# Two plane clears and the natural mask ahead of the first weights' issue on GpSimd, third weights and middle rows behind its first mask

## The chip, the cores and the metric

The kernel runs on one core of a Trainium2 chip. The metric is the device time of one execution in microseconds (us). Five engines work side by side and meet only through semaphores: TensorE (PE in the profile, PEld its weight loads), VectorE (DVE), ScalarE (ACT), GpSimd (POOL) and SyncE (SP), which here only issues transfers. Transfers run on 16 DMA engines that all issuers share: queue 0 holds what GpSimd issues, queue 1 what SyncE issues, queue 10 what ScalarE issues.

## What is computed

Two stages, for 4 batches, 8 heads, 768 tokens, head size 32 and state size 16 (the reference, cut to what matters):

```python
for c in range(24):                       # chunks of 32 tokens, one after the other
    cum = np.cumsum(log_a[chunk], axis=-1)
    M = einsum('bhin,bhjn->bhij', Cc, Bc) * exp(cum_i - cum_j) * causal
    y = einsum('bhij,bhjd->bhid', M, xc)  + einsum('bhin,bhnd->bhid', Cc, state) * exp(cum)
    state = exp(sum(la)) * state + sum_j(Bc * xc * exp(cum_last - cum_j))
x = y.transpose(0, 2, 1, 3).reshape(4 * 768, 256)
out = ((x @ w_a) * (x @ w_b)) @ w_out     # 256 -> 1536 -> 256
```

A scan over the sequence with a decaying state per head, then a bilinear feed-forward network (FFN) on 3072 tokens.

## The kernel before

The sequence is cut into 6 blocks of 128 tokens, each worked on in two pairs of batches, so that there are 12 pairs. Within a block the decay is a running product (`scan`, L250, on VectorE) that is divided by its value in the middle of the block (`over_mid`, L253) and multiplied into B and C. For a pair the scaled B and C are turned so that the state dimension lies on partitions, TensorE forms the scores (`scores`, L404, into four PSUM banks), the scores are multiplied with a causal mask (`mask`: L449 on VectorE, or L446 and L447, a copy by ScalarE and the product by GpSimd), and the masked scores are multiplied with x (`pv_u`, L458). The results are evacuated to X2T (block 0) or XB (later blocks) and go into the FFN: matmuls with Wa and Wb (L598 for block 0, L667 after it), the product of the two (L622, L679), and matmuls with Wo (L637, L693).

The order of the work is written out by hand from L774 on: the kernel takes a manual schedule, each engine carries out its instructions in the order of the text, and a wait holds everything behind it on that engine. Small matmuls on constants (`warmup`, L238) stand between TensorE's pieces in the first 10 us.

*Block 0* (pairs 0 and 1) goes a shorter way than the rest: B and C are loaded by pair, scaled on VectorE (`scale_bc`, L333), turned by TensorE (`transposes`, L374) and copied out (L385, L391). *Pairs 2 and later* use one interleaved buffer each, a plane (three in turn, `planes`), into which GpSimd writes scaled C and B (`scale_q`, L346) and which VectorE turns in one instruction (`turn`, L359). Part of each plane stays zero: `clear` (L294) writes those words once for each of the three planes. The factors of the planes come from the middle rows (`mid_rows`, L288: the running product over its middle value, on GpSimd), which VectorE turns (`turned_rows`, L297) and which are copied into FC and inverted into FB.

There are two masks. `causal` (L222, L225) is in the order of the first two blocks, whose tokens are interleaved by two; `causal_q` (L915, L916) is in natural order and is used from pair 4 on.

*Loads.* ScalarE and SyncE issue B and C of block 0 first, GpSimd issues x of pair 0 (L153), the first halves of Wa and Wb (L185), x of pair 1, then the second halves; Wa's second half ("third weights") at L234, ahead of everything that GpSimd computes, and Wb's second half ("fourth") at L814. The weights are converted to 16 bits by the transfer. SyncE then issues the eight loads of block 1 (`load_q`, L164: four of C into cq, four of B into bq), with a dependency written by hand on the first half of Wa, so that they don't start ahead of it (L815, L816). The loads of x and B for pairs 2 and 3 follow.

*PSUM banks.* Two double banks hold scores. Four more (ff0 to ff3) are handed out in order of use by the string `BANKS`; its first entries are, in order, fps, tb, tc, py0, py1, then three results with Wa and three with Wb for pair 0. A bank that is handed out again makes the new writer wait for the readers of the old content.

Of the kernel before, what the change touches and what calls it, by code (L numbers as in the profile page):

```python
# [12 lines left out]
u32 = mybir.dt.uint32  # L13
AF = mybir.ActivationFunctionType
ALU = mybir.AluOpType
# [4 lines left out]
SS = 64.0  # L20

BANKS = (
    "012313213212312312031203123021032103120312013201320130231021302130231203120312013023102310"
    "2312013201320132012301230123012301230123012301320132013201320132013201320132013201320"
)


# [1 line left out]
def kernel(  # L29
# [13 lines left out]
    nc = tc.nc  # L43
# [3 lines left out]
    Q = 128  # L47
# [30 lines left out]
    Wa = [big.tile([128, 2, KC], f16, name=f"Wa{t}") for t in range(2)]  # L78
# [6 lines left out]
    causal_q = big.tile([128, Q], f16, name="causal_q")  # L85
# [10 lines left out]
    planes = [big.tile([128, 288, 4], f16, name=f"planes{t}") for t in range(NR)]  # L96
# [32 lines left out]
    def bank(name):  # L129
        return psf.tile([128, 512], f32, name=name, tag=f"ff{next(banks)}")  # L130
# [12 lines left out]
    def load1(eng, p, which, bt, i0=0, n=64, to=None):  # L143
        blk, bp = divmod(p, NBP)
        if p >= P2:
            return eng.dma_start(
                by_token(pair_in[p][which])[:, bt],
                (B, C, x)[which][2 * bp + bt, :, blk * Q : (blk + 1) * Q, :].rearrange("h q n -> q h n"),
            )
        src = (B, C, x)[which][2 * bp + bt, :, blk * Q + 2 * i0 : blk * Q + 2 * i0 + 2 * n, :]  # L150
        if to is None:
            to = pair_in[p][which]
        return eng.dma_start(  # L153
            to[64 * bt + i0 : 64 * bt + i0 + n].rearrange("i h r n -> i h (r n)"),
            src.rearrange("h (i r) n -> i h (r n)", r=2),
        )
# [3 lines left out]
    def load_q(eng, blk, parts=ALL_Q):  # L160
        if blk not in by_batch:
            by_batch[blk] = [inq.tile([128, H, 4, N], f32, name=n_, tag=n_) for n_ in ("bq", "cq")]
        return [
            eng.dma_start(  # L164
                by_batch[blk][w][32 * b : 32 * b + 32].rearrange("i h s n -> i h (s n)"),
                (B, C)[w][b, :, blk * Q : (blk + 1) * Q, :].rearrange("h (i s) n -> i h (s n)", s=4),
            )
            for w, b in parts
        ]
# [12 lines left out]
    def load_w(half, W):  # L182
        src = moe_w_a if W is Wa else moe_w_b
        c = slice(half * KC, (half + 1) * KC)
        return nc.gpsimd.dma_start(W[half], src.rearrange("(f p) e -> p f e", p=128)[:, :, c])  # L185

    def load_wo(half):
# [2 lines left out]
            moe_w_out.rearrange("(g p kk) e -> p g (kk e)", p=128, kk=3)[:, 2 * half : 2 * half + 2],  # L190
        )

    nc.sync.dma_start(a_sb, a.rearrange("b h (k q) -> (b h) k q", q=Q))
    for p_ in range(2):
        tiles(p_)
# [5 lines left out]
    for w in (1, 0):  # L201
# [6 lines left out]
        out=ident, in_=ident, compare_op=ALU.is_equal, fill=0.0, base=0, pattern=[[-1, 128]], channel_multiplier=1  # L208
# [14 lines left out]
    for bt in range(2):  # L223
        v = causal[64 * bt : 64 * bt + 64]
        nc.gpsimd.affine_select(  # L225
            out=v, in_=v, compare_op=ALU.is_ge, fill=0.0, base=0, pattern=[[-1, 2], [1, Q]], channel_multiplier=-2
        )
    for p in range(2):
        for bt in range(2):
            load1(nc.gpsimd, p, 2, bt)  # L230
        if p == 0:
            w0 = load_w(0, Wa)
            load_w(0, Wb)
    load_w(1, Wa)  # L234

    def warmup(bank, *widths):
        for cols in widths:
            nc.tensor.matmul(  # L238
                bank[:, 0:cols],
                nc.const_aps.tensor(1.0, [128, 128], mybir.dt.bfloat16),  # L240
                nc.const_aps.tensor(1.0, [128, cols], mybir.dt.bfloat16),
                start=True,
                stop=True,
                skip_group_check=True,
            )


    def scan(lo, hi):
        for k in range(lo, hi):
            nc.vector.tensor_tensor_scan(Pr[:, k], a_sb[:, k], zero, 1.0, ALU.mult, ALU.add)  # L250
# [4 lines left out]
    def sel_over_mid(lo, hi, eng):  # L255
        eng.tensor_tensor(
            out=selr[:, lo:hi].rearrange("p k t c -> p k (t c)"),
            in0=sel.rearrange("p t b h -> p (t b h)").unsqueeze(1).broadcast_to((BH, hi - lo, 2 * NBP * H)),
            in1=rmid[:, lo:hi].unsqueeze(2).broadcast_to((BH, hi - lo, 2 * NBP * H)),
            op=ALU.mult,  # L260
        )
# [24 lines left out]
    def mid_rows(lo, hi, eng):  # L286
        k = slice(lo + NBLK - NT, hi + NBLK - NT)
        eng.tensor_tensor(  # L288
            out=Ps[:, lo:hi], in0=Pr[:, k], in1=rmid[:, k].unsqueeze(2).broadcast_to((BH, hi - lo, Q)), op=ALU.mult
        )  # L290

    def clear(t_, eng):
        words = t_.rearrange("p c s -> p (c s)").bitcast(u32).rearrange("p (g w) -> p g w", g=3)
        eng.memset(words[:, 0:2, 32:96], 0)  # L294

    def turned_rows(lo, hi):
        nc.vector.transpose(  # L297
# [26 lines left out]
    def scale_bc(p, which, eng, factor=None):  # L324
        blk, bp = divmod(p, NBP)
        name, f = (("bm", fB), ("cm", fC))[which]
        if p >= P2:
            f = (fBl, fCl)[which][:, blk - P2 // NBP].rearrange("p (b t h) -> p b t h", b=NBP, t=2)[:, bp]
        else:
            f = f[:, blk, :, bp]  # L330
        raw = by_token(pair_in[p][which]) if p >= P2 else pair_in[p][which].rearrange("p h r n -> p r h n")
        m_ = mid.tile([128, 2, H, N], f16, name=name, tag=name)
        eng.tensor_tensor(  # L333
            out=m_,
            in0=raw,
            in1=(f if factor is None else factor).unsqueeze(3).broadcast_to((128, 2, H, N)),
            op=ALU.mult,
        )
        st.setdefault(p, {})[name] = m_
# [94 lines left out]
    def product0(m2, e):  # L434

        return (
            st[0]["T1"][:, 2 * m2 : 2 * m2 + 2].rearrange("p m (e r) q -> p e m (r q)", e=2)[:, e],
            (SC0, SC1)[m2][:, :, e * 256 : e * 256 + 256],
            causal.rearrange("p r q -> p (r q)").unsqueeze(1).broadcast_to((128, 2, 2 * Q)),
        )  # L440

    def mask(out_in, by_pool=False):
        o_, i_, c_ = out_in
        if by_pool:
            tmp = mid.tile([128, *c_.shape[1:]], f32, name="tmp", tag="tmp")
            nc.scalar.copy(tmp, i_)  # L446
            nc.gpsimd.tensor_tensor(out=o_, in0=tmp, in1=c_, op=ALU.mult)  # L447
        else:
            nc.vector.tensor_tensor(out=o_, in0=i_, in1=c_, op=ALU.mult)  # L449

    def pv_u(p, u, py, first):
        s = st[p]
        for r in range(2):
            for g in range(4):
                for bt in range(2):
                    h = u * 4 + g
                    k = slice(64 * bt, 64 * bt + 64)
                    nc.tensor.matmul(  # L458
                        py[bt][32 * g : 32 * g + 32, u * Q : (u + 1) * Q],
                        s["X16"][k, h, r, :],  # L460
                        s["T1"][k, h // 2, h % 2 * 2 + r],
                        start=(first and u == 0 and r == 0),
                        stop=(r == 1),
                        skip_group_check=True,
                        tile_position=(64 * bt, 32 * g),
                    )
# [93 lines left out]
    def evac0(u, bt, eng, py):  # L560
        o_, i_ = X2T[:, 0, bt, u], py[bt][:, u * Q : (u + 1) * Q]
        if eng is nc.scalar:
            nc.scalar.activation(out=o_, in_=i_, func=AF.Copy, scale=YS / SS)
        else:
            nc.vector.tensor_scalar(o_, i_, YS / SS, None, ALU.mult)
# [218 lines left out]
    scale_bc(0, 1, nc.vector, v.rearrange("p (r b h) -> p r b h", r=2, b=NBP)[:, :, 0])  # L784
    over_mid(1, 2)
    sel_over_mid(1, 2, nc.vector)
    mid_rows(0, 1, nc.gpsimd)
    tb, tcp = bank("tb"), bank("tc")
    transposes(0, [tb, tcp], lambda: warmup(SC[3], 256))
    nc.scalar.copy(flat(fC, 0, 1), v)  # L790
# [3 lines left out]
    mask(product0(0, 0))  # L794
    mask(product0(0, 1))
    mask(product0(1, 1), by_pool=True)
    mask(product0(1, 0))
    clear(planes[0], nc.gpsimd)
    warmup(tcp, 512)
    factors_mm(1, 2, fps, 1)  # L800
    warmup(tcp, 512, 512)
# [3 lines left out]
        evac0(0, bt, nc.scalar, py)  # L805
    warmup(tcp, 512, 128)
    scale_bc(1, 1, nc.vector)
    scan(4, 5)
    scale_bc(1, 0, nc.vector)
    clear(planes[1], nc.gpsimd)  # L810
    pv_u(0, 1, py, True)
    for bt in range(2):
        evac0(1, bt, (nc.scalar, nc.vector)[bt], py)
    load_w(1, Wb)  # L814
    for i_ in load_q(nc.sync, 1):  # L815
        tc.add_manual_dep(i_.ins, w0.ins.name, AFTER, reason="first weights ahead of block 1")  # L816
    for p in (2, 3):
# [2 lines left out]
    for p in (2, 3):  # L820
# [10 lines left out]
        out=hsx,  # L831
# [11 lines left out]
    for m in range(3):  # L843
# [37 lines left out]
        out=Ge.rearrange("p k (g e) -> p g k e", e=2),  # L881
# [8 lines left out]
    for (p, k2), a_sb_ in zip(late, asb):  # L890
# [21 lines left out]
    batch_factors(1, 2, 2, 3)  # L912
    scale_bc(2, 0, nc.gpsimd)
    scale_bc(3, 0, nc.gpsimd)
    nc.gpsimd.memset(causal_q, SS)  # L915
    nc.gpsimd.affine_select(  # L916
        out=causal_q, in_=causal_q, compare_op=ALU.is_ge, fill=0.0, base=0, pattern=[[1, Q]], channel_multiplier=-1
    )
    for m in range(3):
        mask(product(3, m))  # L920
    batch_inverse(1, 2)
# [6 lines left out]
    for c in range(3):  # L928
        p, bt = divmod(c, NBP)
# [137 lines left out]
```

## Time and profile before

| | |
|---|---|
| runs shown: median (lowest to highest) | 122.97 us (122.58 to 123.0) |
| profiled execution: its own time | 122.69 us |
| its span | 120.8 us |
| busy: PE, DVE, ACT, POOL | 96%, 75%, 56%, 49% of the span |
| granted TensorE clock | 1.0 throughout |
| DMA engines' busy share, by fortieths of the span (3.02 us each) | 0.3 in the first, 0.9 or more in the next seven |

All times inside the profile count from the start of the span. Its time lines give start, length, engine, line, operation, written and read tiles, and in brackets how long the engine was idle before and what ended that. A busy PE is not one at its peak, since matmuls overlap and their ends are modelled; a wait is put down to the last of several semaphores. The three busiest groups outside TensorE, for the scale of things (line, engine, operation, tiles, shapes, count, then busy us, mean ns of one, and idle us before it):

```profile
L612 ACT COPY asb<-aps 128x512 f32<-128x512 f32 x72 | 42.0, 587 | 17.2 <-PE aps L667 13.4
L679 DVE TENSOR_TENSOR hkb<-bps,asb 128x512 f16<-128x512 f32 x60 | 40.2, 687 | 12.7 <-ACT asb L612 11.1
L449 DVE TENSOR_TENSOR t<-SC,causal_q 128x512 f16<-128x512 f32 x27 | 17.3, 681 | 2.4 <-PE SC L404 2.4
```

### The profile page before, as it was taken

What the parts mean: (1) busy time and instruction counts of PE and PEld (TensorE: products, weight loads), DVE (VectorE), ACT (ScalarE), POOL (GpSimd) and SP (SyncE); (2) the same over time, 40 slices, a digit from 0 to 9 for tenths busy, and PEclk for the clock granted to TensorE, in tenths of its full rate; (3) what the DMA queues carried; (4) which work ended last, traced back from release to release, by engine and by line L of the source; (5) the groups of instructions that cost most, each with busy time, mean ns of one, the idle gap of its engine ahead of it and who ended that gap; (6) DMA issues with size and microseconds to landing.
All of it is one profiled execution on the core that took longest, in us unless ns stands there. A gap on an engine that the chain in (4) does not pass through costs nothing.

```text
span 120.8 us, 3551 instructions
## 1 busy us (share of the span) xinstructions
PE 115.9 (96%) x1385; PEld 73.9 (61%) x1386; DVE 90.2 (75%) x166; ACT 67.9 (56%) x136; POOL 58.8 (49%) x92
## 2 busy tenths in 40 slices
PE   7989999999999999999999999999999999999990
PEld 2436789888644488544485464775465684645880
DVE  5998988999798994599966999686899426758000
ACT  0446756769776646567666646635735637475230
POOL 7994986999699969387803994200000000000000
PEclk9999999999999999999999999999999999999999
DMA  3999999894789994959992929012001111010132
GB/s 63 135 183 192 207 230 197 134 200 113 99 94 161 115 139 101 110 68 121 218 241 89 85 9 121 5 46 87 5 6 40 43 49 44 0 43 0 43 108 71
DMA packets 59297, 12.13 MB, mean 100 GB/s; under 512 B 54480, under 2 KB 59216, under 8 KB 59280
## 3 DMA queue, kind: packets, MB, share of 16 engines
q0 software_dynamic: 20320, 3.80, 38.9%
q1 hardware_dynamic: 36432, 7.74, 34.8%
q10 hardware_dynamic: 2528, 0.36, 1.8%
q8 instruction: 11, 0.18, 0.7%
q14 instruction: 6, 0.05, 0.1%
HBM read 12.42 MB, written 3.15 MB: 129 GB/s over the span
## 4 chain that ended last, share of the span: by engine, by line
PE 92%; DVE 4%; issue 0%; ACT 0%
PE ops L693 22%; PE aps L667 22%; PE bps L667 21%; PE ops L637 5%; PE aps L598 4%; PE SC L404 4%; PE bps L598 3%; DVE t L449 3%; PE SC L238 3%; PE SC L473 2%; PE SC L536 1%; PE tc L238 1%; PE py L458 1%; PE SC L485 1%; DVE bt L385 1%
## 5 line engine op out<-in xcount | busy, mean ns | idle before, releaser
L612 ACT COPY asb<-aps 128x512 f32<-128x512 f32 x72 | 42.0, 587 | 17.2 <-PE aps L667 13.4
L679 DVE TENSOR_TENSOR hkb<-bps,asb 128x512 f16<-128x512 f32 x60 | 40.2, 687 | 12.7 <-ACT asb L612 11.1
L667 PE MATMUL aps<-XB,Wa 128*128 128x512 f16 x120 | 35.7, 379 | 0.0
L667 PE MATMUL bps<-XB,Wb 128*128 128x512 f16 x120 | 35.7, 379 | 0.0
L693 PE MATMUL ops<-Wo,hkb 128*128 128x256 f16 (+1 forms) x252 | 28.1, 268 | 0.0
L693 PEld LDWEIGHTS <-hkb 128*128 128x128 f16 x252 | 23.0, 98 | 3.8
L667 PEld LDWEIGHTS <-Wb 128*128 128x128 f16 x120 | 12.4, 103 | 13.6
L667 PEld LDWEIGHTS <-Wa 128*128 128x128 f16 x120 | 12.1, 103 | 11.7 <-issue 0.5
L449 DVE TENSOR_TENSOR t<-SC,causal_q 128x512 f16<-128x512 f32 x27 | 17.3, 681 | 2.4 <-PE SC L404 2.4
L705 ACT ACTIVATE osb<-ops 128x256 f32<-128x256 f32 (+1 forms) x20 | 7.6, 379 | 18.4 <-PE ops L693 18.4
L447 POOL TENSOR_TENSOR t<-tmp,causal_q 128x512 f16<-128x512 f32 x5 | 5.8, 1161 | 10.0 <-ACT tmp L446 10.0
L177 POOL DMA_DIRECT2D xn<-in_x_dram x8 | 9.5, 1192 | 0.0
L346 POOL TENSOR_TENSOR planes<-cq,FC 128x256 f16<-128x256 f32 x10 | 7.6, 775 | 2.2 <-DMA cq<-in_C_dram 2.1
L622 DVE TENSOR_TENSOR hk<-bps,asb 128x512 f16<-128x512 f32 x11 | 7.2, 672 | 0.9 <-ACT asb L612 0.8
L346 POOL TENSOR_TENSOR planes<-bq,FB 128x256 f16<-128x256 f32 x10 | 7.7, 772 | 0.4 <-DMA bq<-in_B_dram 0.4
L449 DVE TENSOR_TENSOR t<-SC,causal 128x512 f16<-128x512 f32 x11 | 7.0, 675 | 0.4 <-PE SC L404 0.3
L598 PE MATMUL aps<-X2T,Wa 128*128 128x256 f16 x48 | 6.8, 274 | 0.0
L446 ACT COPY tmp<-SC 128x512 f32<-128x512 f32 x10 | 5.9, 589 | 1.5 <-PE SC L404 1.1
L598 PE MATMUL bps<-X2T,Wb 128*128 128x256 f16 x48 | 6.6, 273 | 0.0
L558 ACT ACTIVATE XB<-SC 128x512 f16<-128x512 f32 (+1 forms) x9 | 4.6, 547 | 3.5 <-PE SC L501 2.4
L447 POOL TENSOR_TENSOR t<-tmp,causal 128x512 f16<-128x512 f32 x5 | 5.8, 1161 | 0.0
L637 PE MATMUL ops<-Wo,hk 128*128 128x256 f16 x48 | 5.8, 273 | 0.0
(101 smaller groups left out, 109.2 us busy)
## 6 DMA issues: line engine op xcount, KB each, us to landing
out_dram<-osb SPq DMA_DIRECT2D x23, 128.0 KB, 1.8
cq<-in_C_dram SPq DMA_DIRECT2D x20, 64.0 KB, 3.9
bq<-in_B_dram SPq DMA_DIRECT2D x18, 64.0 KB, 3.8
bn<-in_B_dram SPq DMA_DIRECT2D x8, 128.0 KB, 4.1
xn<-in_x_dram POOLq DMA_DIRECT2D x8, 128.0 KB, 5.9
Wa<-in_moe_w_a_dram POOLq DMA_DIRECT2D x2, 384.0 KB, 7.3
Wb<-in_moe_w_b_dram POOLq DMA_DIRECT2D x2, 384.0 KB, 7.9
Wo<-in_moe_w_out_dram POOLq DMA_DIRECT2D x2, 384.0 KB, 6.5
```

Of the source, the lines that this page charges most:

```text
L177: eng.dma_start(by_token(pair_in[p][which]).rearrange("p t h n -> p (t h) n"), src.rearrange("t h q n -> q (t h) n"))
L346: eng.tensor_tensor(out=plane[:, c0 : c0 + 4 * step].rearrange("p (j c) s -> p j s c", c=step)[:, :, :, 0:N], in0=by_batch[blk][which][:, ...
L447: nc.gpsimd.tensor_tensor(out=o_, in0=tmp, in1=c_, op=ALU.mult)
L449: nc.vector.tensor_tensor(out=o_, in0=i_, in1=c_, op=ALU.mult)
L598: nc.tensor.matmul(ps[:, kk * 2 * Q : (kk + 1) * 2 * Q], W[k // 6][:, f, k % 6 // 3 * 384 : (k % 6 // 3 + 1) * 384].rearrange("p (c kk) -> ...
L612: (nc.vector.tensor_copy if on_dve else nc.scalar.copy)(asb, a_ps)
L622: eng.tensor_tensor(out=s["hk"][:, 2 * k2 : 2 * k2 + 2, :].rearrange("p k q -> p (k q)"), in0=b_ps, in1=asb, op=ALU.mult)
L637: nc.tensor.matmul(o_ps[:, 0:d_model], hk[:, k, bt * Q : (bt + 1) * Q], Wo[:, k, :], start=(k == 0), stop=(k == NK - 1), skip_group_check= ...
L667: nc.tensor.matmul(t_, W[k // 6][:, f, k % 6 // 3 * 384 : (k % 6 // 3 + 1) * 384].rearrange("p (c kk) -> p kk c", kk=3)[:, k % 3], XB[:, b ...
L679: return lambda: nc.vector.tensor_tensor(out=s["hk"][:, k], in0=ps[1], in1=asb, op=ALU.mult)
L693: nc.tensor.matmul(o_ps[:, 0:w], hk[:, k, c * Q : (c + 1) * Q], Wo[:, k, cs], start=(k == 0), stop=(k == NK - 1), skip_group_check=True,)
L705: nc.scalar.activation(out=o_sb[:, 0:w], in_=o_ps[:, 0:w], func=AF.Copy, scale=1.0 / (YS * YS))
```

## The change

Five moves, with no instruction added or taken away:

- GpSimd clears planes 0 and 1 and builds `causal_q` (memset and select) right after x of pair 0, ahead of the first halves of Wa and Wb. Before, the clears stood behind its first mask, and `causal_q` stood ahead of pair 3's masks.
- The third weights go from ahead of GpSimd's computing to behind its first mask. The fourth stay next after the clears' old places and so come right behind the third.
- The middle rows of block 1 go from ahead of the first mask to behind the fourth weights.
- On VectorE the scan of block 4 goes from ahead of pair 1's scaling of B to behind its evacuation of pair 0's second result (L565).
- `BANKS` has other digits. Followed through, all but two handings-out get a bank with the same history as before: the second and the third Wa result of pair 0 exchange theirs (the banks of tc and of py1).

`clear` itself is only moved up in the text.

```diff
--- before.py
+++ after.py
@@ -20,8 +20,8 @@
 SS = 64.0
 
 BANKS = (
-    "012313213212312312031203123021032103120312013201320130231021302130231203120312013023102310"
-    "2312013201320132012301230123012301230123012301320132013201320132013201320132013201320"
+    "012313123121321321032103213012031203210321023102310230132012301230132103210321023013201320"
+    "1321023102310231021302130213021302130213021302310231023102310231023102310231023102310"
 )
 
 
@@ -189,6 +189,10 @@
             Wo[:, 6 * half : 6 * half + 6].rearrange("p (g kk) e -> p g (kk e)", kk=3),
             moe_w_out.rearrange("(g p kk) e -> p g (kk e)", p=128, kk=3)[:, 2 * half : 2 * half + 2],
         )
+
+    def clear(t_, eng):
+        words = t_.rearrange("p c s -> p (c s)").bitcast(u32).rearrange("p (g w) -> p g w", g=3)
+        eng.memset(words[:, 0:2, 32:96], 0)
 
     nc.sync.dma_start(a_sb, a.rearrange("b h (k q) -> (b h) k q", q=Q))
     for p_ in range(2):
@@ -229,9 +233,14 @@
         for bt in range(2):
             load1(nc.gpsimd, p, 2, bt)
         if p == 0:
+            clear(planes[0], nc.gpsimd)
+            clear(planes[1], nc.gpsimd)
+            nc.gpsimd.memset(causal_q, SS)
+            nc.gpsimd.affine_select(
+                out=causal_q, in_=causal_q, compare_op=ALU.is_ge, fill=0.0, base=0, pattern=[[1, Q]], channel_multiplier=-1
+            )
             w0 = load_w(0, Wa)
             load_w(0, Wb)
-    load_w(1, Wa)
 
     def warmup(bank, *widths):
         for cols in widths:
@@ -288,10 +297,6 @@
         eng.tensor_tensor(
             out=Ps[:, lo:hi], in0=Pr[:, k], in1=rmid[:, k].unsqueeze(2).broadcast_to((BH, hi - lo, Q)), op=ALU.mult
         )
-
-    def clear(t_, eng):
-        words = t_.rearrange("p c s -> p (c s)").bitcast(u32).rearrange("p (g w) -> p g w", g=3)
-        eng.memset(words[:, 0:2, 32:96], 0)
 
     def turned_rows(lo, hi):
         nc.vector.transpose(
@@ -784,7 +789,6 @@
     scale_bc(0, 1, nc.vector, v.rearrange("p (r b h) -> p r b h", r=2, b=NBP)[:, :, 0])
     over_mid(1, 2)
     sel_over_mid(1, 2, nc.vector)
-    mid_rows(0, 1, nc.gpsimd)
     tb, tcp = bank("tb"), bank("tc")
     transposes(0, [tb, tcp], lambda: warmup(SC[3], 256))
     nc.scalar.copy(flat(fC, 0, 1), v)
@@ -794,8 +798,8 @@
     mask(product0(0, 0))
     mask(product0(0, 1))
     mask(product0(1, 1), by_pool=True)
+    load_w(1, Wa)
     mask(product0(1, 0))
-    clear(planes[0], nc.gpsimd)
     warmup(tcp, 512)
     factors_mm(1, 2, fps, 1)
     warmup(tcp, 512, 512)
@@ -805,13 +809,13 @@
         evac0(0, bt, nc.scalar, py)
     warmup(tcp, 512, 128)
     scale_bc(1, 1, nc.vector)
-    scan(4, 5)
     scale_bc(1, 0, nc.vector)
-    clear(planes[1], nc.gpsimd)
     pv_u(0, 1, py, True)
     for bt in range(2):
         evac0(1, bt, (nc.scalar, nc.vector)[bt], py)
+    scan(4, 5)
     load_w(1, Wb)
+    mid_rows(0, 1, nc.gpsimd)
     for i_ in load_q(nc.sync, 1):
         tc.add_manual_dep(i_.ins, w0.ins.name, AFTER, reason="first weights ahead of block 1")
     for p in (2, 3):
@@ -912,10 +916,6 @@
     batch_factors(1, 2, 2, 3)
     scale_bc(2, 0, nc.gpsimd)
     scale_bc(3, 0, nc.gpsimd)
-    nc.gpsimd.memset(causal_q, SS)
-    nc.gpsimd.affine_select(
-        out=causal_q, in_=causal_q, compare_op=ALU.is_ge, fill=0.0, base=0, pattern=[[1, Q]], channel_multiplier=-1
-    )
     for m in range(3):
         mask(product(3, m))
     batch_inverse(1, 2)
```

## The prediction

> **What bounds the kernel now.** I read the page first, then the chain of waits in order of time, then GpSimd's and SyncE's own rows, and last the DMA queues in narrow windows, because the change moves four DMA issues. On the page the chain that ended last is TensorE for 92% and VectorE for 4%.
>
> ```profile
> PE 92%; DVE 4%; issue 0%; ACT 0%
> ```
>
> In the chain, VectorE stands almost only before 14 us: from 14.85 on the pieces are TensorE's. So the change can pay or cost in two ways: in the short latency chain before 14 us, and by opening holes in TensorE afterwards. The chain around the change:
>
> ```profile
> 9.21 0.47 PE py L458 x16
> 9.68 0.54 PE tc L238 x2
> 10.22 0.32 PE SC L374 x4
> 10.54 0.87 PE aps L598 x8
> 11.41 0.47 PE SC L404 x32
> 11.88 0.04 issue
> 11.91 1.90 DVE t L449 x3
> ```
>
> To be seen: the first FFN matmuls (aps) want the first weights at 10.4, and the three causal masks of pair 1 are the last VectorE piece. The timeline of GpSimd over the moved stretch (start, length, then line, operation, tiles):
>
> ```profile
> 4.06 0.72 POOL L185 DMA_DIRECT2D Wa<-in_moe_w_a_dram  x1
> 4.76 0.73 POOL L185 DMA_DIRECT2D Wb<-in_moe_w_b_dram  x1
> 5.47 1.41 POOL L153 DMA_DIRECT2D xn<-in_x_dram  x2
> 6.83 0.76 POOL L185 DMA_DIRECT2D Wa<-in_moe_w_a_dram  x1
> 7.65 0.39 POOL L288 TENSOR_TENSOR Ps<-Pr,rmid 32x128 f32<-32x128 f32 x1
> 8.01 1.15 POOL L447 TENSOR_TENSOR t<-tmp,causal 128x512 f16<-128x512 f32 x1
> 9.11 0.34 POOL L294 MEMSET planes<- 128x128 uint32 x2
> 9.40 0.76 POOL L185 DMA_DIRECT2D Wb<-in_moe_w_b_dram  x1
> ```
>
> GpSimd never idles there, so what is put ahead of the first weights delays them in full. Who waits for them: SyncE's list of waits, and GpSimd's.
>
> ```profile
> SPq L164 <- DMA Wa<-in_moe_w_a_dram: 5.1, 1, 5.1
> ```
>
> ```profile
> POOL planes L346 <- DMA cq<-in_C_dram: 1.4, 1, 1.4
> ```
>
> SyncE holds block 1's eight loads until the first weights have landed, and GpSimd's planes wait for them. VectorE's rows show what hangs on the planes:
>
> ```profile
> 19.98 1.29 DVE L622 TENSOR_TENSOR hk<-bps,asb 128x512 f16<-128x512 f32 x2
> 21.34 0.58 DVE L359 STREAM_TRANSPOSE turned<-planes 128x384 f32<-128x384 f32 x1
> 21.84 1.25 DVE L622 TENSOR_TENSOR hk<-bps,asb 128x512 f16<-128x512 f32 x2
> ```
>
> The plane of pair 2 ends at 20.54 + 0.77 = 21.31 on GpSimd; the turn at 21.34 starts on its heels, 0.07 us after VectorE was free (19.98 + 1.29 = 21.27). TensorE's scores of pair 2 begin at 21.98. This is a second anchor of the path, and it hangs on a landing, not on the early chain.
>
> **The change part by part.** The span is 120.8 us and that execution took 122.69 us; the median of the three runs is 122.97, 0.28 above it. Sums are made on 122.69 and moved to the median at the end.
>
> *Ahead of the first weights:* two plane clears (9.11 to the next start at 9.40, 0.29), the mask's memset (29.71 to 29.98, 0.27) and its select (29.98, 0.29). Together 0.85 us: the first weights are issued at 4.91 instead of 4.06, the second at 5.61, and x of pair 1 ends at 7.7 instead of 6.88.
>
> *What that does to the landing.* The first weights landed at 4.06 + 5.8 = 9.86, the second at 4.76 + 7.0 = 11.76. TensorE loads them at 10.32 and 12.05, so there is slack of 0.46 and 0.29. If all 0.85 arrived, both would be late, by 0.39 and 0.56. But queue 0 (GpSimd's) works in order, and x of pair 0 lies ahead of the weights: its 1024 small packets run from 4.2 to about 6.6, and the first large packet moves only then. From an issue's end to its first packet took 0.84 (x: 3.36 to 4.2) and 0.75 (bq: 26.85 to 27.6). The first weights end their issue at 5.63, so they are ready at about 6.4 to 6.5, just before the queue reaches them. From 6.6 to 7.1 they moved little anyway, some 20 large packets against 407 of SyncE's and ScalarE's, and after 7.1 about 12 per 0.1 us; should they come at 7.0, about 20/120 = 0.17 us is lost, less what the other queues finish sooner. Bounds: 0 and 0.85; I take 0.1, by the packets, which leaves both slacks.
>
> *GpSimd's first mask* waits for ScalarE's copy (7.17 + 0.59 = 7.76). The third weights and the middle rows held it until 8.01; now GpSimd is free at 7.7 and the mask runs at 7.78, 0.23 earlier. Worth nothing: the matmuls it feeds were held by another. The first of them runs at 9.21, the rest from 9.38, when ScalarE's second evacuation of the same banks (9.06 + 0.27 = 9.33) had ended; the mask was done at 9.16. Without that cover it would be 0.2.
>
> *Third and fourth weights:* issued at 8.93 and 9.69 instead of 6.83 and 9.40. Queue 0 reaches them at 12.0 and 14.0 (x of pair 1 is before them), ready at 10.5 and 11.25. They landed at 15.7 and 18.1; used at 17.96 and 19.27. Nothing.
>
> *Middle rows* move from 7.65 to about 10.45, read by VectorE at 15.31: 4 us of cover. The third plane's clear moves from 10.15 to about 10.85; GpSimd then idles until 11.87 for VectorE's reciprocal. *The mask taken out at 29.71* frees 0.57 us just before GpSimd waits for a load until 31.01 (0.73 idle). Nothing; without that wait it would advance the planes of pairs 4 and 5, whose turn is at 34.11, with over a microsecond in hand.
>
> *VectorE:* the scan of block 4 goes behind pair 1's scaling and the last evacuation. The scaled B ends at 9.70 + 0.39 = 10.09 and TensorE's transposes start at 10.14; the two warm-ups before them were issued at 9.61 and each streams for about 0.21 (0.61 for two, with about 0.18 of drain), so the array is free at about 10.05. B is now ready at 9.76: **0.09 gained**. The scan then runs from about 10.05 to 10.46, ahead of the copy that starts at 10.58 (then 10.49).
>
> *Banks:* the second and third FFN results swap theirs. The second now takes the bank that VectorE's evacuation frees (10.29 before, about 10.05 after; wanted near 10.9), the third waits for warm-ups long done. Nothing.
>
> *The sum.* 0.09 is gained up to 14 us. It is given back at 21.34: the turn stays where the landing of block 1's loads puts it, and from there VectorE is without a gap until its mask ends at 24.67 + 0.68 = 25.35, when the scores of pair 3 start (25.40). With the landing 0.1 later, 0.1 is lost there; with it sooner, up to 0.07 + 0.09 is kept. I take 0: 122.69, which on the median is 122.97, and call it **122.9**, the middle between the gain kept and the gain lost leaning to the first.
>
> **Where the skill and the trace bear on it.** SyncE issued four loads from 9.85, yet from 9.9 to 13.4 its queue 1 moved nothing:
>
> ```profile
> DMA packets 1432, 0.70 MB, mean 200 GB/s; under 512 B 1072, under 2 KB 1431, under 8 KB 1431
> ...
> q0 software_dynamic: 1431, 0.68, 146.3%
> q8 instruction: 1, 0.02, 1.7%
> ```
>
> Those loads came into motion only as the third weights ran out, as if work were taken in order of arrival. The Trainium skill ("DMA: Bandwidth & Descriptors", "Queues, rings and completion order") has each DMA engine take turns between queues packet by packet. By that rule the loads' place behind the third weights would not matter and the sum would stay at 0. The trace disagrees with it from 9.9 to 13.4 and agrees from 14.0 to 15.5 (171 packets of queue 0 against 165 of queue 1).
>
> The weights' issue also slides under VectorE's two scalings (4.92 to 5.68). The second weights' issue lay there before and took 0.73, against 0.72 to 0.76 elsewhere, so 0. The Trainium skill ("SBUF — State Buffer", "SBUF: two separate sides") warns that VectorE in a two-port mode locks GpSimd out while it writes descriptors. By it the issue could wait until 5.68, up to 0.77 more; the row shows none of it.
>
> **Rivals.**
> *B, slower: the delay is passed on through SyncE.* If the first weights are not ready when x of pair 0 runs out (from 6.6 on each 0.1 us late is 0.1 us), the eight loads behind them start later, the planes move from 19.32, the turn from 21.34 and the scores from 21.98. The full 0.85 gives 123.54 on the profile's time, 123.8 on the median; the holes at 10.3 and 12.05 (0.39, 0.56) lie on the same path and are not added. For it: a saturated queue delayed queue 1 by over 3 us, and descriptors of GpSimd's Wo, issued until 15.86, moved in number only from 17.6. Against it: 0.75 and 0.84 in the two cleaner cases.
> *C, faster: block 1's loads overtake the third weights.* Those now become ready at about 10.5, as late as SyncE's loads (9.85, plus 0.7 as the first load of all took). If arrival decides, the loads start at 12.0 instead of 13.5, and the planes no longer hold the turn: 0.16, 122.8 on the median. The bound is all of TensorE's idle time until 31.49: 72 FFN matmuls at 0.109, 48 output ones at 0.109 and 2.6 of scores and states make 15.7 of 16.64 us, so under 0.95 in all, 122.0.
> *The move is idle* is part of the forecast: the order of both kernels' instructions shows that GpSimd's and VectorE's moves are real and nothing else moved.
>
> **How the numbers follow.** Forecast (within 0.3 of the median, 122.6 to 123.2): 0.50. B: 0.30, of it 0.22 beyond 0.61 us. C: 0.20, of it 0.10 beyond. 0.5% is 0.61 us, about what a measurement of this kernel can tell from no change. So faster 0.10, within 0.68, slower 0.22. The range goes from 122.3 (C, two thirds of its bound) to 123.85 (B in full).
>
> **What would show it.** Right: the first weights' issue at 4.9, SyncE's first load of block 1 at 9.8 to 10.1, GpSimd's mask at 7.8 with matmuls still from 9.38, transposes near 10.05, the turn of pair 2 near 21.3. B: SyncE's load after 10.4 and TensorE waiting at the first or second weights or at scores of pair 2. C: queue 1 moving before 13 us and no idle before the planes. Wrong altogether: a hole in TensorE after 31.5, where I see no path from the change.

## The result, and the profile after

The changed kernel took 124.16 us in the median (123.46 to 126.6, 9 runs) beside 123.0 us before (122.58 to 123.31, 9 runs): a ratio of 1.0081, 95% interval 1.006 to 1.0101. Measured again beside the experiments, the same kernel came out at 1.0026 (1.0004 to 1.0048) and at 1.0041 (1.0011 to 1.007). It is slower each time; the first and the second interval do not overlap, and that stays open below. Some executions of any of these kernels take 1.5% and more longer (as the 126.6 here), the ratios leave them out, and of the profiles below the one of the fourth experiment is from such an execution and the one with the weights first in their queue may be. The first profiled execution took 123.58 us with a span of 121.9, against 122.69 and 120.8 before.

The page's chain by engine, to be held against the one of before:

```profile
PE 85%; DMA 5%; POOL 4%; DVE 3%; issue 1%; ACT 0%; DVEq 0%; POOLq 0%
```

A transfer and GpSimd are now in it. The chain in order of time (start, length, what) shows where, and that the moved instructions themselves are links of it:

```profile
4.09 0.35 POOL planes L195 x2
4.44 0.15 POOL causal_q L238
4.59 0.07 issue
4.65 0.24 POOL causal_q L239
4.89 5.67 DMA Wa<-in_moe_w_a_dram
10.56 0.05 issue
10.61 1.05 PE aps L603 x8
...
21.57 0.77 POOL planes L351
22.34 0.02 issue
22.37 0.59 DVE turned L364
22.96 0.04 issue
23.00 0.65 PE SC L409 x32
```

The first weights are issued at 4.89 and land at 10.56 (9.83 before; the prediction's 9.86 is 4.06 and a rounded 5.8); TensorE stands still for them from 10.32, for 0.29. The plane of pair 2 ends at 22.34 (21.31), its turn starts at 22.37 (21.34), its scores at 23.00 (21.98). From there both kernels run alike: the first large FFN matmul of block 1 starts at 32.36 against 31.33, and the spans differ by 1.0. SyncE's and GpSimd's lists of waits carry the same:

```profile
SPq L164 <- DMA Wa<-in_moe_w_a_dram: 5.9, 1, 5.9
```

```profile
POOL planes L351 <- DMA cq<-in_C_dram: 2.3, 2, 2.0
```

SyncE waits 0.8 longer for the first weights, GpSimd up to 2.0 instead of 1.4 for block 1's C. The other two traces of the changed kernel (the second and third measurement) have the same hole in front of the scores of pair 2. Scores of pair 2 in the three:

```profile
23.00 0.65 PE L409 MATMUL SC<-turned 32*64 32x128 f16 x32 [0.70 <-DVE turned L364]
22.88 0.65 PE L409 MATMUL SC<-turned 32*64 32x128 f16 x32 [0.56 <-DVE turned L364]
23.88 0.65 PE L409 MATMUL SC<-turned 32*64 32x128 f16 x32 [1.05 <-DVE turned L364]
```

In front of its first matmul on the first weights TensorE waits 0.29, 0.04 and 0.76 in the three. The kernel before has neither wait. What the other moves were to do came about. GpSimd's timeline, behind x of pair 1:

```profile
7.71 1.19 POOL L452 TENSOR_TENSOR t<-tmp,causal 128x512 f16<-128x512 f32 x1
8.81 0.76 POOL L185 DMA_DIRECT2D Wa<-in_moe_w_a_dram  x1
9.56 0.71 POOL L185 DMA_DIRECT2D Wb<-in_moe_w_b_dram  x1
10.28 0.42 POOL L297 TENSOR_TENSOR Ps<-Pr,rmid 32x128 f32<-32x128 f32 x1
```

The mask starts 0.30 sooner, and the transposes of pair 1 (they turn the scaled B and C) start at 9.93 instead of 10.14. It does not help, since the first weights come at 10.56.

**Where the time was lost: the DMA engines between 7 and 8 us.** What moved in that microsecond, for the kernel before (queue, packets, MB, share of 16 engines):

```profile
DMA packets 210, 0.19 MB, mean 185 GB/s; under 512 B 97, under 2 KB 210, under 8 KB 210
...
q0 software_dynamic: 113, 0.17, 99.9%
```

and for the changed kernel, with the engines' busy tenths by fortieths of the window ahead of it:

```profile
DMA  9995944954454462339511448040490606093600
...
DMA packets 309, 0.07 MB, mean 73 GB/s; under 512 B 284, under 2 KB 309, under 8 KB 309
...
q0 software_dynamic: 44, 0.04, 64.4%
```

Queue 0 moved 0.04 MB instead of 0.17. In the second half the engines are idle for long stretches: x of pair 0 has gone through (its last packet ends at 7.36), and the weights, whose issue ended 1.4 to 2.4 us earlier, are not yet under way. Lost there is 0.13 MB, about 0.7 us at the pace of the queue (0.1 MB per half microsecond). By the page the engines are 0.9 or more busy in each fortieth of the span from 3 to 24 us, so there is little room to make it good.

These two executions are the extremes, though. By 8.0 us 112 large packets of queue 0 had ended in the kernel before and 21 in the changed one. The other four traces with the first weights issued at 4.06 have 72 to 106, the other five with them issued at 4.9 have 46 to 67. On average that is 40 packets or 0.06 MB, about 0.3 us.

### The profile page after: what moved, and what is told of

It reads as the page before. It is cut to its first block, busy times and chain, and to the rows that moved or that the text cites. A ratio compares the mean times of both kernels' runs of the same rounds, so it can differ in the third digit from the quotient of the medians.

```text
span 121.9 us, 3550 instructions
## 1 busy us (share of the span) xinstructions
PE 115.9 (95%) x1386; PEld 73.7 (61%) x1386; DVE 90.2 (74%) x166; ACT 67.8 (56%) x136; POOL 58.7 (48%) x92
## 4 chain that ended last, share of the span: by engine, by line
PE 85%; DMA 5%; POOL 4%; DVE 3%; issue 1%; ACT 0%; DVEq 0%; POOLq 0%
PE ops L698 22%; PE aps L672 22%; PE bps L672 21%; DMA Wa<-in_moe_w_a_dram 5%; PE ops L642 4%; PE SC L409 4%; PE aps L603 4%; PE bps L603 2%; PE SC L478 2%; DVE t L454 2%; POOL xn L153 1%; PE SC L541 1%; DVE hk L627 1%; POOL causal L229 1%; POOL planes L351 1%
## 5 line engine op out<-in xcount | busy, mean ns | idle before, releaser
L672 PEld LDWEIGHTS <-Wa 128*128 128x128 f16 x120 | 12.1, 103 | 11.7 <-issue 0.5
L364 DVE STREAM_TRANSPOSE turned<-planes 128x384 f32<-128x384 f32 x10 | 5.5, 562 | 0.8 <-POOL planes L351 0.8
```

The costliest lines, as they stand in the source:

```text
L672: nc.tensor.matmul(t_, W[k // 6][:, f, k % 6 // 3 * 384 : (k % 6 // 3 + 1) * 384].rearrange("p (c kk) -> p kk c", kk=3)[:, k % 3], XB[:, b ...
```

## The experiments

Times are ratios to the kernel before on the same chip, with 95% intervals. "Last packet" is the time at which 256 large packets of queue 0 have ended, counted in the packet records of each trace. The first weights are 256 packets, but the second follow in the same queue, so this shows the pace of the queue. The landing, which the waits hang on, came 0.6 to 1.25 us after it.

**Only what stands ahead of the first weights** (third weights, middle rows, scan and banks as before):

```diff
         if p == 0:
+            clear(planes[0], nc.gpsimd)
+            clear(planes[1], nc.gpsimd)
+            nc.gpsimd.memset(causal_q, SS)
+            nc.gpsimd.affine_select(
...
             w0 = load_w(0, Wa)
```

> The kernel before with one part of the change: the two plane clears and the natural mask stand ahead of the first weights; third weights, middle rows, the scan and the banks stay as they were. Theory (the first weights' issue is late by 0.85 us, the transfers start late by as much, and all that queues behind them, block 1's loads and with them the planes of pair 2, moves along): first weights land near 10.6, planes of pair 2 start near 20.3, time +0.8 to +1.2 us on before, as the whole change. Rival (the third weights or the middle rows behind the first mask cost the time): within 0.3 us of before.

Measured: 1.0036 (1.0016 to 1.0057), 123.41 us. +0.44 us lies between the two: a loss, but half of the theory's. Last packet at 9.46, planes at 19.02: this execution's planes were not late at all, and its early chain was. The early chain in this trace, GpSimd, VectorE and TensorE:

```profile
8.79 1.18 POOL L453 TENSOR_TENSOR t<-tmp,causal 128x512 f16<-128x512 f32 x1
9.36 0.90 DVE L339 TENSOR_TENSOR cm<-cn,fC 128x256 f16<-128x256 f32 x1
10.96 0.28 PE L380 MATMUL SC<-ident,bm 128*128 128x128 f16 x2
```

and VectorE's row in the kernel before:

```profile
8.99 0.46 DVE L333 TENSOR_TENSOR cm<-cn,fC 128x256 f16<-128x256 f32 x1
```

Here the third weights and the middle rows still stand ahead of GpSimd's first mask, so the four instructions push that mask from 8.01 to 8.79. VectorE's scaling of C, which now lies under the mask, takes 0.90 instead of 0.46, the transposes start 0.82 later and the first FFN matmul at 11.20 instead of 10.38. The weights had landed at 10.30 by then, and the turn of pair 2 starts without a wait for its plane. A second trace of the same kernel (the last round below) shows the same: mask at 8.81, scaling of C 1.11, transposes at 10.98, first FFN matmul at 11.21, weights landed at 10.23, no wait at the turn. So in both traces this kernel loses on another path than late weights, and one that the changed kernel does not have: there the mask starts at 7.71. Its time is no measure of what the late weights cost.

**The same four instructions behind x of pair 1, the rest as changed:**

```diff
-            clear(planes[0], nc.gpsimd)
...
             w0 = load_w(0, Wa)
             load_w(0, Wb)
+    clear(planes[0], nc.gpsimd)
+    clear(planes[1], nc.gpsimd)
+    nc.gpsimd.memset(causal_q, SS)
+    nc.gpsimd.affine_select(
```

> The changed kernel with the two clears and the natural mask taken from ahead of the first weights and put behind x of pair 1, where GpSimd would idle until its first mask; third and fourth weights, middle rows and scan stay as changed. Theory: the first weights are issued at 4.06 again, land at 9.8 to 9.9, planes of pair 2 start by 19.4, and the time is that of before, -0.2 to +0.1 us (the 0.09 us that the transposes start sooner can be kept only if the planes come sooner too). Rival (third weights behind the mask cost the time): still +0.6 us or more on before.

Measured: 1.0007 (0.9984 to 1.003), 123.18 us. In time as the theory had it: with the first weights issued at 4.05 again, the late third weights and middle rows cost nothing that can be told, which leaves room for up to 0.3%. Its GpSimd timeline shows that the block fits into a gap:

```profile
5.45 1.41 POOL L153 DMA_DIRECT2D xn<-in_x_dram  x2
6.90 0.35 POOL L195 MEMSET planes<- 128x128 uint32 x2
7.19 0.20 POOL L240 MEMSET causal_q<- 128x128 f16 x1
7.46 0.29 POOL L241 TENSOR_SCALAR_AFFINE_SELECT causal_q<-causal_q 128x128 f16<-128x128 f16 x1
7.83 1.16 POOL L452 TENSOR_TENSOR t<-tmp,causal 128x512 f16<-128x512 f32 x1
```

The numbers of the expectation were not all met: planes at 19.92 where 19.4 was expected, with SyncE's first load at 10.40. The first weights landed 0.5 us later than in the profile of before (10.38), though they were issued at the same time. The three further traces with that issue have 10.27, 10.30 and 10.46, so the 9.83 of the profile before is the quick one. And the scores of pair 2 wait in this trace too:

```profile
22.92 0.65 PE L409 MATMUL SC<-turned 32*64 32x128 f16 x32 [0.43 <-DVE turned L364]
```

The hole in front of them thus does not need the delay of the first weights. That the late third and fourth weights hold back block 1's loads is a rival that this experiment does not exclude.

**Block 1's loads released by GpSimd's first mask:**

```diff
-    mask(product0(1, 1), by_pool=True)
+    m0 = mask(product0(1, 1), by_pool=True)
...
-        tc.add_manual_dep(i_.ins, w0.ins.name, AFTER, reason="first weights ahead of block 1")
+        tc.add_manual_dep(i_.ins, m0.ins.name, AFTER, reason="first weights ahead of block 1")
```

(`mask` also returns GpSimd's instruction.)

> The changed kernel, in which block 1's eight loads are held back by GpSimd's first mask (end near 8.9) and no longer by the first weights (10.56). Theory (the loss is passed on through the late loads of block 1, the holes in TensorE at 10.3 and 12.1 lie on the same path and alone are worth 0.25): planes of pair 2 no longer hold the turn, which starts near 21.5, and the time falls to +0.2 to +0.5 us on before. Rival (the holes in front of the first and second weights are the loss): no gain, or a loss, since the loads now compete with the weights: +0.9 us or more on before.

Measured: 1.0014 (0.9985 to 1.0042), 123.25 us. The turn starts at 21.89, later than the expected 21.5, and still waits 0.30 for the plane. The median is 0.17 us above before by the ratio, just under the theory's range, but the interval takes in both no loss and the change's 1.0026 and 1.0041, so it leans and does not decide.

**A third of the delay** (clears ahead, `causal_q` back at its old place):

> The changed kernel with only the two clears ahead of the first weights (0.29 us of delay for 0.85) and the natural mask at its old place ahead of pair 3's masks. Theory (each tenth of delay of the issue arrives at the loads and planes): first weights land near 10.1, planes start near 19.65, time +0.2 to +0.4 us on before. Rival, as the prediction had it (the weights are ready before their queue reaches them, so that a small delay is free): first weights land at 9.9 as before and the time is within 0.15 us of before.

Measured: 1.0017 (0.9991 to 1.0043), and not decided by the time. The packets speak for the rival: issued at 4.39, the first weights had their last packet at 9.31, within the 9.14 to 9.49 of the undelayed kernels. The landing does not: 10.22 is nearer the theory's 10.1 than the rival's 9.9, and it too lies within the 9.83 to 10.46 of the undelayed kernels. So this is not decided.

**The change again, twice the delay, both cures, and the weights first in their queue.** The edits: none; the four instructions written twice in a row; the second and third experiment together; and, in the kernel before,

```diff
+    w0 = load_w(0, Wa)
     for p in range(2):
         for bt in range(2):
             load1(nc.gpsimd, p, 2, bt)
         if p == 0:
-            w0 = load_w(0, Wa)
             load_w(0, Wb)
```

> The changed kernel unaltered, beside the other kernels of this list on one chip. The four kernels above lie at +0.1 to +0.45 us, the whole change at +1.0, and the parts do not add up to it (0.45 for what is ahead of the first weights, 0.1 for the rest). Theory (the parts do add up, and the rest is spread between executions): +0.4 to +0.7 us on before. Rival (the late third weights make the delay of the first ones dearer): +0.8 to +1.2 us again.

> The changed kernel with the two clears and the natural mask built twice in a row ahead of the first weights: 1.7 us of delay for 0.85. Theory (what the weights come too late for their queue is lost one for one; the first 0.85 is partly hidden behind x of pair 0, whose packets run until 6.5 to 6.8, the second not at all): first weights land near 11.4, the planes near 21.2, and the time is +0.8 to +0.95 us on the changed kernel. Rival (the path is held by something else than the weights' issue): less than +0.4 us on the changed kernel.

> Both cures together: the clears and the natural mask behind x of pair 1 (first weights issued at 4.06), and block 1's loads released by GpSimd's first mask (near 8.95) and no longer by the first weights. Theory: loads ahead of the third weights in the DMA engines, planes of pair 2 before 19.0, no hole at the first weights, the sooner transposes kept: -0.1 to -0.3 us on before. Rival (the loads take the DMA engines from the first and second weights and the gain is given back there): 0 to +0.3 us on before.

> The kernel before with the first weights issued ahead of x of pair 0 (near 2.5 instead of 4.06), to see by itself how long they take from issue to motion with nothing ahead in their queue. Prediction's value, 0.75 to 0.85 us from the end of the issue: first large packets in number near 4.1. Rival (2.3 us, as the first weights and Wo show when taken at face value): near 5.5. The time is not of interest; x of pair 0 comes later and the time should be +0.5 to +2 us.

The change again: 1.0026 (1.0004 to 1.0048), 123.4 us. That 0.36% and 0.07% from the first two experiments add up to about as much shows nothing, as the first of them loses on a path of its own. Twice the delay: 1.0096 (1.0067 to 1.0125), 0.70% or 0.86 us more than the change beside it, for 0.80 us more delay: one for one within the intervals, which leave some 0.45 us either way. A loss from the delay itself is clear of noise here. The landing came out sooner than expected, 11.0 for 11.4, and the last packet at 10.41. The plane of pair 2, second half, starts at 22.36 after 1.16 us of waiting; the profile names VectorE, whose factors had long been done, and the last of block 1's B loads landed at 22.15. In the kernel before the same step starts at 20.54, 0.21 after that landing (20.33), in the changed one at 21.57 (21.35): it is the last B load that lets this step start, and the turn follows it. TensorE waits 0.22 for the first weights and the turn 1.15 for its plane in this trace, so the loss here lies with the landings. What moved from 7 to 8 us in that kernel:

```profile
DMA  8576459999111119990090000000000000000099
...
DMA packets 217, 0.05 MB, mean 53 GB/s; under 512 B 198, under 2 KB 217, under 8 KB 217
...
q0 software_dynamic: 24, 0.03, 102.8%
```

For half a microsecond the DMA engines do nothing. The weights' issue ended at 6.43; the first large packets start at 7.15, 0.72 later, and are still in flight (24 packets with a share of 102.8%) when all else is done.

Both cures: 0.9987 (0.997 to 1.0003), clear of the change's 1.0026 beside it: in this round they take the loss away. The weights first in their queue, kernel before, from 4.2 to 5.2 us:

```profile
DMA  9999749979392992911990009000000000000490
...
DMA packets 315, 0.07 MB, mean 73 GB/s; under 512 B 290, under 2 KB 315, under 8 KB 315
...
q0 software_dynamic: 25, 0.04, 113.6%
```

The issue runs from 2.51 to 3.40. By the packet records the first large packet starts at 4.26, 0.86 after its end; that was the prediction's value. But 14 of the first twenty packets take 0.6 to 1.6 us, where later ones take 0.13. The eighth has ended at 5.17, the sixteenth at 5.30, the 64th at 5.96. So neither value of the expectation (4.1 and 5.5), though the rival's is the nearer: the weights are *begun* 0.86 us and *under way* some 1.8 to 1.9 us after their issue has ended. This one execution took 126.28 us, 3.2 over the kernel before, where 0.5 to 2 had been expected; that stays open.

**A last round for the sizes:** the change, its first part and both cures again, and the kernel before with only the loads released by the mask.

> The changed kernel a third time, since its first and second measurement lie apart (+0.81% with an interval of 0.60 to 1.01, then +0.26% with 0.04 to 0.48). Theory (the loss is the part of the first weights' delay that x of pair 0 does not hide, and this part varies from execution to execution with the end of x's packets): +0.3 to +0.7 us on before, first weights' packets at full pace near 7.5 to 8.0 against 7.2. Rival (the first measurement is the rule): +0.8 to +1.2 us.

> The kernel before with only the two clears and the natural mask ahead of the first weights, again, for a narrower interval beside the whole change on the same chip. Theory (this part is the whole loss): within 0.25 us of the changed kernel, +0.3 to +0.6 us on before. Rival (the rest of the change has a cost of its own): at least 0.3 us below the changed kernel.

> Clears and mask behind x of pair 1, block 1's loads released by GpSimd's first mask, again (first measurement -0.13%, interval -0.30 to +0.03). Theory: -0.1 to -0.3 us on before. Rival (no gain: what the loads win the weights lose): within 0.1 us of before.

> The kernel before with one line changed: block 1's loads are released by GpSimd's first mask (end 9.16) and no longer by the first weights (9.86). The third weights are issued at 6.8, ahead of the loads, so that the loads stay behind them in the DMA engines. Theory (the loads' place among the weights decides, not their issue): planes of pair 2 within 0.4 us of 19.3 and the time within 0.15 us of before. Rival (each tenth of an earlier issue arrives): planes near 18.6, -0.2 us on before.

Measured: the change 1.0041 (1.0011 to 1.007), its first part 1.003 (1.0013 to 1.0047), 0.14 us apart. That the first part alone costs about as much as the change is what the expectation asked for, but it is met by luck: by its traces that kernel loses at the mask and not at the weights. Both cures 1.0015 (0.9987 to 1.0042): with the first measurement on the other side of 1, no gain over before is shown, and no version here beats it; against the change beside it the intervals now overlap. The kernel before with its loads released sooner: 1.0002 (0.9983 to 1.0022), planes at 18.90, at the edge of what the theory allowed; an earlier issue of the loads buys nothing that can be told.

The landing against the delay, all traces together:

| delay of the first weights' issue | last packet, mean (range, traces) | landing, mean (range) | time to before |
|---|---|---|---|
| 0 | 9.31 (9.14 to 9.49, 5) | 10.25 (9.83 to 10.46) | 1.0002 to 1.0015 and 0.9987 |
| 0.33 | 9.31 (1) | 10.22 | 1.0017 |
| 0.85 | 9.70 (9.46 to 9.94, 6) | 10.52 (10.23 to 11.08) | 1.0014 (loads released by the mask), else 1.0026 to 1.0081 |
| 1.65 | 10.41 (1) | 11.01 | 1.0096 |

Of the 0.85 some 0.3 to 0.4 arrives, of the next 0.80 some 0.5 to 0.7; that the 0.33 was hidden rests on one trace. The landings of the first and third rows overlap. From SyncE's first load on, which starts as the weights land, the lateness is handed on in full: in the ten traces in which SyncE's loads do not overtake the third weights, queue 1's first packet follows that issue by 3.5 to 3.9 us (9.27 to 12.96, 9.85 to 13.70, 10.58 to 14.30 and 11.09 to 14.76, for instance).

## Why the prediction was wrong, point by point

- **What bounds the kernel: right.** The chain, the slack of 0.46 and 0.29 at the weights, SyncE's wait and the second anchor at the turn of pair 2 are what the change ran into.
- **The delay of the issue, 0.85: right** (4.89 against 4.06 is 0.83).
- **What the delay does to the landing: this is the step that failed.** The prediction took the weights to be "ready at about 6.4 to 6.5", 0.75 to 0.84 after the issue's end, "just before the queue reaches them", and took 0.1 of the bounds 0 and 0.85. The first packet indeed starts at 6.56. But the 0.75 to 0.84 was read off other transfers: x, whose packets are 128 bytes and take 0.03 us, and bq, 16 packets of 4096 bytes that take 0.16 to 0.22 from the first one on (by the packet records that first one comes at 27.74, 0.89 after the issue's end). The weights' first packets can take up to 1.6 us (in the two traces of the first experiment none of the first twenty is over 0.5, so this differs between executions). In seven of the eight traces with the first weights issued at 4.9 or later, or first in their queue, sixteen large packets have ended 1.7 to 1.9 us after the issue's end (2.3 in the first profile of the change). So the weights are under way at about 7.4, when 1000 of x's 1024 packets have been gone for 0.4 to 0.8 us. With the issue ending at 4.78 the same 1.8 us end at about 6.6, as the 1000th packet of x does (6.60 in the kernel before, where x's last ends at 6.88 and not at 6.6). The right row was in the text, among B's reasons: Wo's issue ended at 15.86 and it "moved in number only from 17.6". It is the same kind of transfer, and was put below two rows of another kind because these were "cleaner". The term measured 0.39 on average by the last packet (9.31 to 9.70) and 0.27 by the landing (10.25 to 10.52), not 0.1.
- **The sum of 0: wrong by that term.** Rival B, at 0.30, named the mechanism and its place; its price, 0.85, was that of the whole delay, and what arrived was +1.0 us in the first measurement and +0.3 and +0.5 in the later ones. By the prediction's own rule (0.1 later at the landing is 0.1 lost at the turn) the measured term gives 0.3 to 0.4, which fits the later two; the first stays unexplained. The signs that it named for B came in all three traces of the change: SyncE's first load after 10.4, waits at the first weights and at the scores of pair 2.
- **Nothing for the mask, the third and fourth weights, the middle rows, the clears and the banks: right** as far as the time of the second experiment tells (1.0007, interval 0.9984 to 1.003). For the third and fourth weights it is not settled: the last of block 1's B loads landed at 20.16 to 21.09 in the five traces with the third weights ahead of GpSimd's first mask, and at 20.86 to 22.24 in the eight with them behind it (the fourth experiment is left out), with the first weights delayed or not. The transposes' 0.09 came (9.93 against 10.05 expected, with the whole early chain 0.13 sooner in that execution) and was lost at the weights.
- **Rival C: loads can overtake, but its price is wrong.** Where block 1's loads were issued before the third weights' issue had ended, queue 1 moved from 11.5 to 11.9 on; where they came after it, only from 12.1 to 14.8, 3.5 to 3.9 us after their issue instead of 1.4 to 2.7. In the changed kernel, from 10.7 to 14.1:

```profile
DMA packets 1411, 0.67 MB, mean 196 GB/s; under 512 B 1072, under 2 KB 1410, under 8 KB 1410
...
q0 software_dynamic: 1410, 0.65, 145.9%
```

  SyncE's loads, issued from 10.58 on, have no packet in it. But once overtaking, they share the engines with the weights, and the last of the four C loads landed at 19.41 and 19.38 (third experiment, both cures again), no sooner than the 19.16 of before. The Trainium skill ("DMA: Bandwidth & Descriptors", "Queues, rings and completion order") has the queues take turns packet by packet; the traces agree with it once both are under way (171 packets of queue 0 to 165 of queue 1 from 14.0 to 15.5 in the kernel before), and not while transfers issued earlier are ahead (1410 to none above).
- **VectorE locking out the weights' issue: rightly set at 0.** The issue now lies under VectorE's two scalings (4.79 to 5.55) and took 0.72, as before. The Trainium skill's warning ("SBUF — State Buffer", "SBUF: two separate sides") is of VectorE in a two-port mode. Its effect is not seen here, and no run shows whether these two scalings are in such a mode, so the 0.77 that the prediction worked out by it has no ground.
- **The chances.** The interval of the forecast rested on one profiled execution that was a quick one (122.69 where the median is 123.0): its first weights landed at 9.83, while the four other traces with the same issue had them at 10.27 to 10.46. Slack of 0.46 read off such an execution is not slack in all of them.

**What stays open.** Why the change cost 0.81% in the first measurement and 0.26% and 0.41% in the other two, with intervals that partly exclude each other, was not settled. The three traces of the changed kernel have their last packet at 9.94, 9.63 and 9.83 and SyncE's first load at 10.58, 10.49 and 11.09, while their first weights landed at 10.56, 10.47 and 11.08. So the landing varies by more than half a microsecond within one kernel; whether the chip has a part in it is not shown. How the loss splits between the late first weights and the late third and fourth ones is open too. Doubling the delay shows that the first weights' issue costs time, and both cures together removed the loss in one of two rounds, but no run has the first weights late, the third and fourth at their old place and the mask not held up. Why the first packets of a weights' transfer take up to 1.6 us was not tried either.

## What to carry to other kernels

Work put ahead of a DMA issue can be free only while the queue is still busy with earlier transfers when the new one is truly under way. Take that time from a transfer of the same kind and size, and count to where its packets flow, not to where the first one starts. If an engine has a gap a few instructions further on, as GpSimd had behind x of pair 1, try the work there: here it cost nothing that could be told. Read slack off several executions, since a landing here moves by half a microsecond from one to the next. And when a part of a change is run alone, check in its trace that it loses where the whole change loses: here the part alone held up a mask that the change had moved out of the way.

## What was not expected of the hardware

The start of a large converting transfer is slow: with nothing ahead of it in its queue the first packet follows the issue's end by 0.72 us (twice the delay) and 0.86 (weights first), then 20 and 14 of the first twenty packets of 1536 bytes take 0.6 to 1.6 us against 0.13 later, and with nothing else queued the DMA engines idle meanwhile. Loads that overtake weights start 1.4 to 2.7 us after their issue instead of 3.5 to 3.9, and land no sooner than in the kernel before.
